# Decode attention with a gated MLP on one core: moving the output selection behind K's second turn, P's copies between the turns, head maxima onto VectorE

## The chip, the cores and the metric

The kernel runs on 1 core of one Trainium2 chip. The metric is device microseconds of a run, as a median of several runs. Besides that time there is one profiled execution of each kernel, whose "span" (first to last instruction) is about 2 us shorter than the run's time.

Engines in the profile: PE is TensorE (matmul), PEld its weight loads, DVE is VectorE, ACT is ScalarE, POOL is GpSimd, SPq is the SyncE queue that issues the loads. QK(g) is the product of the queries with K tile g, PV(g) the product of the softmax's result P with V tile g; PSUM is the memory that the matmuls write (psb in the lines); the kernel uses it in banks. A batch boundary is the step from one batch's last K tile to the next batch's first.

## The reference, cut to what matters

```python
# x: 4 x 1 x 576; 32 query heads, 16 KV heads, head size 128; window of 4096 of 16384 positions
q = layernorm(x) @ wq
k = k_cache[:, :, -4096:, :]; v = v_cache[:, :, -4096:, :]     # each KV head serves two query heads
p = softmax((q @ k.T) * 128 ** -0.5)
h = x + (p @ v) @ wo
gate, up = layernorm(h) @ W_gate, layernorm(h) @ W_up          # 576 x 4608
out = h + (relu(gate) * up) @ W_down
```

All weights and caches are bf16. The window of K and V is 4 batches x 16 heads x 4096 x 128 x 2 bytes x 2, that is 134 MB of the 159.8 MB that the profile counts. Each is used once, so the work is a stream of loads.

## The kernel before: the parts that the change touches

K and V come in 16 tiles each of 4 MiB: tile g has the four KV heads `4*(g%4)` and up of batch `g//4`. They go into four slots, in the order K(g), V(g-4), K(g+1), V(g-3) and so on. So K(g) takes the slot of K(g-2) and its load can be issued only when QK(g-2) has finished; V(g-4) takes the slot of V(g-6) and waits for PV(g-6).

A K tile is turned by VectorE (the kernel's addressing takes a turn as a transposition of blocks of 32x32), in place and in two halves of 128x4096 f32 that take 4.43 us each, before QK can use it:

```python
def turn_k(g, w):                       # w: which half
    ...
    dve(("TRA", g, w), lambda e: e.transpose(out=dst, in_=src), [("L", "K", g)] if w == 0 else [])
def pe_qk(g):   # 32 matmuls; waits for ("TRA", g, 1); of a new batch also for EXP, MAX, EV of the old one
    ...
```

After a batch's fourth QK the softmax follows. The kernel takes the maximum of each row on VectorE and then the maximum over the four rows of a head: with a matmul that lays the 128 maxima in one row, a reduction, a copy, and another matmul that spreads them again:

```python
def head_max(b):
    pe (("MT", b), ... matmul(m_ps[0:1, 0:128], lhsT=stat[:, b, 0:1], rhs=ident_f) ..., [("MAX", b), ...])
    dve(("GM", b), ... tensor_reduce(min) ...);  dve(("GM1", b), ... tensor_copy ...)
    pe (("MB", b), ... matmul(m_ps[:, 0:1], lhsT=gm4[0:1, :], rhs=scl[0:1, 0:1]) ..., [("GM1", b), "c_scl"])
    dve(("NB", b), ... tensor_copy(out=stat[:, b, 1:2], in_=m_ps[:, 0:1]) ..., [("MB", b)])
```

`exps` then computes P, VectorE turns it, `remap` moves it with 16 small matmuls and copies the result to `pT` (four copies on ScalarE, `EV 0`; four on VectorE, `EV 1`). PV(g) multiplies P with a V tile into four PSUM banks; `select_o(g)` picks the wanted entries out of these banks: two products from PSUM (`OSD`), one from SBUF (`OS`), one sum (`OSEL`). PV(g+1) waits for `OSD(g)`, as it writes the same banks. `weights(b)` computes the softmax's divisors once per batch, with two matmuls. The order in which all this is put in the engines' queues is the loop:

```python
def do_v(g):
    pe_pv(g)
    if qd == 0: late.append(lambda: weights(b))
    late.append(lambda: select_o(g))
for g in range(NTILE):
    turn_k(g, 0)
    if g == 4:
        soft(0); remap(0)
    flush()                              # runs what is in late: the selection of V tile g-5
    turn_k(g, 1)
    pe_qk(g)
    if g % 4 == 3 and g > 3: soft(g // 4)
    if g >= 4: do_v(g - 4)
    if g % 4 == 3 and g > 3: remap(g // 4)
for g in range(NTILE - 4, NTILE):
    do_v(g); flush()
```

In the traces below the instructions of an engine start in this order (K7's second turn starts behind the selection at 134.64 us, though its data were there at 122.52), so a place in the order is a possible wait.

## Time and profile before

| | before |
|---|---|
| time, median of 3 runs (range) | 405.31 us (403.62 to 405.83) |
| span of the profiled execution | 403.2 us |
| bytes, mean rate over the span | 159.8 MB, 396 GB/s |
| busy: TensorE, VectorE, ScalarE | 216.4, 228.0, 54.2 us |

No engine is busy for more than 57% of the span. The page's two rows over 40 slices of 10.08 us show what DMA does, first as busy tenths, then as GB/s:

```profile
DMA  9999999999999999769999999399999997999990
GB/s 361 419 416 462 418 419 452 429 419 434 440 423 423 452 421 419 325 260 416 410 427 424 436 423 436 128 419 413 423 423 436 434 429 328 395 417 411 418 403 10
```

The row is near 425 except for the slices 17 and 18 (325 and 260), 26 (128) and 34 (328), counted from 1, and the ends. Cutting the span at these places gives the table of stretches (columns: from and to, length, busy time and number of instructions of each engine, granted TensorE clock with 1.00 as full speed, DMA share, GB/s):

```profile
core 0: us, PE busy (x) PEld busy (x) DVE busy (x) ACT busy (x) POOL busy (x), PEclk, DMA share, GB/s
10.00:168.50 158.50, 69.88 (x476) 11.70 (x236) 106.33 (x69) 25.01 (x35) 7.84 (x13) 0.75 1.00 430
168.50:176.00 7.50, 6.06 (x42) 0.94 (x19) 5.76 (x3) 0.00 (x0) 0.00 (x0) 0.63 0.24 79
176.00:253.50 77.50, 40.16 (x240) 6.01 (x101) 46.48 (x37) 8.49 (x16) 0.00 (x0) 0.77 0.99 424
253.50:262.50 9.00, 6.12 (x43) 0.81 (x19) 7.20 (x3) 0.00 (x0) 0.00 (x0) 0.67 0.27 93
262.50:341.00 78.50, 48.65 (x265) 6.91 (x108) 40.71 (x36) 8.49 (x16) 0.00 (x0) 0.80 0.98 420
341.00:345.20 4.20, 1.99 (x11) 0.78 (x5) 1.96 (x6) 1.16 (x2) 0.00 (x0) 0.94 0.54 164
...
392.80:403.20 10.40, 6.11 (x87) 4.39 (x87) 2.17 (x6) 0.98 (x2) 0.00 (x0) 0.98 0.04 13
```

There are three holes, with 79, 93 and 164 GB/s. The chain that ended last is the list of work, each step released by the one before, that leads to the last instruction. Its first line gives shares by engine, its second by line of the program:

```profile
PE 50%; DVE 36%; DMA 12%; issue 1%; ACT 0%; SPq 0%; DVEq 0%
PE psb L34 29%; DVE sb_arena L442 18%; DMA sb_arena<-in_A_k_cache_dram 12%; PE psb L530 8%; PE psb L466 6%; DVE sb_o_tmp L543 5%; DVE sb_o_sel L547 3%; DVE sb_pp L508 3%; DVE sb_o_tmp L546 2%; DVE sb_stat L471 1%; PE psb L726 1%; PE psb L497 1%; PE psb L646 1%; PE psb L688 1%; PE psb L638 0%
```

DMA has only 12% of this chain; TensorE (PV is at lines 34 and 530, QK at 34 and 466) and VectorE (turn at 442, selection at 543 to 547, P's copies at 508) have 86%. VectorE's timeline around the first batch boundary at which PV runs too, K7 to K8 (called the first from here on; K11 to K12 is the second), shows the chain (columns: start in us, duration, what; in brackets the idle time before it and what ended that):

```profile
122.52 4.45 DVE L442 STREAM_TRANSPOSE sb_arena<-sb_arena 128x4096 f32<-128x4096 f32 x1 [1.91 <-DMA sb_arena<-in_A_k_cache_dram]
131.57 1.38 DVE L543 TENSOR_TENSOR sb_o_tmp<-psb,sb_fm 32x512 f32<-32x512 f32 x2 [4.61 <-PE psb L34]
...
134.64 4.44 DVE L442 STREAM_TRANSPOSE sb_arena<-sb_arena 128x4096 f32<-128x4096 f32 x1
143.03 1.23 DVE L471 TENSOR_REDUCE sb_stat<-psb 128x1 f32<-128x1024 f32 x1 [3.96 <-PE psb L34]
...
155.42 2.73 DVE L508 TENSOR_SCALAR sb_pp<-psb,sb_m 128x512 bf16<-128x512 f32 x4 [7.31 <-PE psb L497]
158.07 4.43 DVE L442 STREAM_TRANSPOSE sb_arena<-sb_arena 128x4096 f32<-128x4096 f32 x1
162.43 1.34 DVE L543 TENSOR_TENSOR sb_o_tmp<-psb,sb_fm 32x512 f32<-32x512 f32 x2
...
165.45 8.76 DVE L442 STREAM_TRANSPOSE sb_arena<-sb_arena 128x4096 f32<-128x4096 f32 x2
```

From 122.52 us: K7's first half is turned as soon as it lands. The selection of V2 waits for PV(2) until 131.57, and only then comes the turn of K7's second half, although K7 had landed twelve us earlier. QK(7) follows and ends at 143.03. P's copies then start at 155.42, after 7.31 us of waiting for the remap, which stands behind PV(3) on TensorE. Only after them come K8's turn, another selection, and the second turn. The line `x2` at 165.45 is K8's second half and K9's first.

The load queue shows the price (columns: start in us, time to issue, what). K10's load waits for QK(8) and leaves at 173.90, 31 us after K9's, and the queue ran dry at about 168.5:

```profile
143.02 0.53 SPq L247 DMA_DIRECT2D sb_arena<-in_A_k_cache_dram  x1
...
173.90 0.53 SPq L247 DMA_DIRECT2D sb_arena<-in_A_k_cache_dram  x1
```

TensorE's timeline at the same place shows the two small matmuls of the head maxima (lines 475 and 482) between QK and PV:

```profile
142.31 0.68 PE L34 MATMUL psb<-sb_arena 128*32 128x512 bf16 x4
144.31 0.38 PE L475 MATMUL psb<-sb_ident_f,sb_stat 128*1 128x128 f32 x2 [1.32 <-DVE sb_stat L471]
145.31 0.38 PE L482 MATMUL psb<-sb_scl,sb_gm 1*128 1x1 f32 x2 [0.62 <-DVE sb_gm L480]
145.62 0.39 PE L530 MATMUL psb<-sb_arena,sb_pp 128*128 128x512 bf16 x1
...
146.71 1.47 PE L34 MATMUL psb<-sb_arena,sb_pp 128*128 128x512 bf16 x3
...
150.98 0.81 PE L34 MATMUL psb<-sb_arena,sb_pp 128*128 128x512 bf16 x3
```

QK ends at 143.0 and PV starts at 145.62, 2.6 us later. Some of PV's matmuls, from 146.7 to 150.1 us, then ran at half the rate: 1.47 us against 0.81 us for three.

From the list of waits (columns: who waited for whom, us in total, times, longest), VectorE waits mostly for TensorE and hardly for loads:

```profile
DVE sb_o_tmp L543 <- PE psb L34: 54.7, 9, 7.0
DVE sb_arena L442 <- DMA sb_arena<-in_A_k_cache_dram: 12.2, 8, 2.4
```

The 72 matmuls of the down projection run without a break at the end, so they waited for computing and not for their weights:

```profile
395.55 4.59 PE L726 MATMUL psb<-sb_arena,sb_pp 128*32 128x288 bf16 x72
```

### The profile page before, as it was taken

Reading aid. Unit: us, or ns where it says so; the run is one execution under the profiler, and the core shown is the slowest. Engines: PE = TensorE matmul, PEld = TensorE weight load, DVE = VectorE, ACT = ScalarE, POOL = GpSimd, SP = SyncE. Lnnn points to the kernel's source line nnn. Section 1 sums busy time; section 2 is a strip of 40 time slices with the busy share of each in tenths; the row PEclk is TensorE's granted clock in tenths of the full one; section 3 lists DMA queues with packets and bytes.
Section 4 is the critical chain, followed back from the end, with each engine's and each line's share of the span. In section 5 each row is a group of like instructions: output and inputs, shape, how many; then the busy total and the mean of one; then the engine's idle time right before and its main releaser. Section 6 shows DMA issues by size and latency. Waiting matters only on the chain.

```text
span 403.2 us, 2703 instructions
## 1 busy us (share of the span) xinstructions
PE 216.4 (54%) x1495; PEld 40.9 (10%) x727; DVE 228.0 (57%) x202; ACT 54.2 (13%) x89; POOL 16.2 (4%) x39
## 2 busy tenths in 40 slices
PE   0403334182829284191927380555473768787676
PEld 0100000010101010010100010010010101100424
DVE  3279978756574735939393629838466322334221
ACT  3290000301010113000001013010101130012110
POOL 8700000000000000000000000000000000000000
PEclk9956886577779779586869596686879698899769
DMA  9999999999999999769999999399999997999990
GB/s 361 419 416 462 418 419 452 429 419 434 440 423 423 452 421 419 325 260 416 410 427 424 436 423 436 128 419 413 423 423 436 434 429 328 395 417 411 418 403 10
DMA packets 6660, 159.76 MB, mean 396 GB/s; under 512 B 748, under 2 KB 888, under 8 KB 1528
## 3 DMA queue, kind: packets, MB, share of 16 engines
q1 hardware_dynamic: 6632, 159.59, 93.0%
q8 instruction: 9, 0.15, 0.1%
q14 instruction: 3, 0.02, 0.0%
q10 hardware_dynamic: 16, 0.01, 0.0%
HBM read 159.58 MB, written 0.00 MB: 396 GB/s over the span
## 4 chain that ended last, share of the span: by engine, by line
PE 50%; DVE 36%; DMA 12%; issue 1%; ACT 0%; SPq 0%; DVEq 0%
PE psb L34 29%; DVE sb_arena L442 18%; DMA sb_arena<-in_A_k_cache_dram 12%; PE psb L530 8%; PE psb L466 6%; DVE sb_o_tmp L543 5%; DVE sb_o_sel L547 3%; DVE sb_pp L508 3%; DVE sb_o_tmp L546 2%; DVE sb_stat L471 1%; PE psb L726 1%; PE psb L497 1%; PE psb L646 1%; PE psb L688 1%; PE psb L638 0%
## 5 line engine op out<-in xcount | busy, mean ns | idle before, releaser
L442 DVE STREAM_TRANSPOSE sb_arena<-sb_arena 128x4096 f32<-128x4096 f32 x32 | 141.0, 4430 | 12.2 <-DMA sb_arena<-in_A_k_cache_dram 12.2
L466 PE MATMUL psb<-sb_arena 128*32 128x512 bf16 x256 | 42.2, 628 | 137.4 <-DVE sb_arena L442 137.4
L34 PE MATMUL psb<-sb_arena,sb_pp 128*128 128x512 bf16 x384 | 108.9, 394 | 0.0
L530 PE MATMUL psb<-sb_arena,sb_pp 128*128 128x512 bf16 x128 | 50.9, 398 | 9.3 <-DVE sb_o_tmp L543 9.3
L543 DVE TENSOR_TENSOR sb_o_tmp<-psb,sb_fm 32x512 f32<-32x512 f32 x32 | 21.7, 678 | 55.0 <-PE psb L34 54.7
L540 ACT COPY sb_o_tmp<-psb 32x512 f32<-32x512 f32 x32 | 18.5, 578 | 204.5 <-PE psb L34 204.2
L34 PE MATMUL psb<-sb_arena 128*32 128x512 bf16 x256 | 44.1, 652 | 0.0
L466 PEld LDWEIGHTS psb<-sb_arena 128*32 128x32 bf16 x256 | 9.7, 120 | 179.6 <-DVE sb_arena L442 150.6
L530 PEld LDWEIGHTS psb<-sb_arena,sb_pp 128*128 128x128 bf16 x128 | 12.9, 101 | 113.6 <-issue 113.6
L508 DVE TENSOR_SCALAR sb_pp<-psb,sb_m 128x512 bf16<-128x512 f32 x16 | 10.9, 744 | 21.5 <-PE psb L497 21.5
L547 DVE TENSOR_REDUCE sb_o_sel<-sb_o_tmp 128x128 f32<-128x512 f32 x16 | 16.3, 1021 | 0.5
L487 ACT ACTIVATE sb_pp<-psb,sb_stat 128x512 bf16<-128x512 f32 x8 | 5.4, 683 | 80.7 <-DVE sb_stat L483 80.7
L556 DVE RECIPROCAL sb_stat<-psb 128x1 f32<-128x1 f32 x4 | 0.7, 168 | 25.9 <-PE psb L554 25.9
L511 ACT ACTIVATE sb_pp<-psb,sb_m 128x512 bf16<-128x512 f32 x16 | 9.7, 688 | 22.7 <-PE psb L497 22.7
L471 DVE TENSOR_REDUCE sb_stat<-psb 128x1 f32<-128x1024 f32 x4 | 4.9, 1225 | 11.9 <-PE psb L34 11.9
L546 DVE TENSOR_TENSOR sb_o_tmp<-sb_o_tmp,sb_fm 64x512 f32<-64x512 f32 x16 | 11.0, 689 | 0.5
L433 ACT COPY sb_arena<-sb_q_keep 32x256 bf16<-32x256 bf16 x8 | 9.7, 1450 | 0.1
L491 DVE STREAM_TRANSPOSE sb_pp<-sb_pp 128x512 bf16<-128x512 bf16 x8 | 5.5, 711 | 3.4 <-ACT sb_pp L487 3.4
L419 DVE CAST sb_pp<-psb 128x512 bf16<-128x512 f32 x1 | 2.4, 2426 | 8.3 <-PE psb L398 8.3
L34 PE MATMUL psb<-sb_arena,sb_hnT 128*32 128x384 bf16 x80 | 6.0, 383 | 0.0
L497 PE MATMUL psb<-sb_pp,sb_to_v 128*32 128x256 bf16 x64 | 4.3, 402 | 2.5 <-DVE sb_pp L491 2.5
L688 PE MATMUL psb<-sb_arena,sb_hnT 128*32 128x384 bf16 x40 | 4.0, 383 | 2.2 <-DVE sb_hnT L669 2.2
(135 smaller groups left out, 95.1 us busy)
## 6 DMA issues: line engine op xcount, KB each, us to landing
sb_arena<-in_A_k_cache_dram SPq DMA_DIRECT2D x16, 4096.0 KB, 17.2
sb_arena<-in_A_v_cache_dram SPq DMA_DIRECT2D x16, 4096.0 KB, 16.8
sb_arena<-in_A_wo_dram SPq DMA_DIRECT2D x1, 4608.0 KB, 13.6
sb_arena<-in_B_W_gate_dram SPq DMA_DIRECT2D x1, 4608.0 KB, 15.9
sb_arena<-in_A_wq_dram SPq DMA_DIRECT2D x1, 4096.0 KB, 12.2
sb_arena<-in_B_W_down_dram SPq DMA_DIRECT2D x3, 1296.0 KB, 19.8
sb_arena<-in_B_W_up_dram SPq DMA_DIRECT2D x1, 3456.0 KB, 16.7
sb_arena<-in_B_W_up_dram SPq DMA_DIRECT2D x1, 1152.0 KB, 19.1
```

The lines of the kernel that those rows point to most:

```text
L34: return e.add_instruction(mybir.InstMatmult(name=e.bass.get_next_instruction_name(), engine=mybir.EngineType.PE, ins=[e.lower_ap(rhs), e. ...
L433: act("QW", lambda e, i=i, q=q: e.copy(out=bass.AP(tensor=arena, offset=32 * i * AW + 2 * i + q, ap=[[AW, 32], [512, 16], [136, 4], [32, 4]]),
L442: dve(("TRA", g, w), lambda e: e.transpose(out=dst, in_=src), [("L", "K", g)] if w == 0 else [])
L466: fn = lambda e, out_=out_, lhsT=lhsT, rhs=rhs, start=start, stop=stop: e.matmul(out_, lhsT=lhsT, rhs=rhs, start=start, stop=stop, skip_gr ...
L471: dve(("MAX", b), lambda e: e.tensor_reduce(out=stat[:, b, 0:1], in_=psb[:, 0:2, :].rearrange("p a b -> p (a b)"), axis=AX.X, op=ALU.max, ...
L508: dve(("EV", b, 1), lambda e, out_=out_, src=src, a=a: e.tensor_scalar(out=out_, in0=src, scalar1=m4[:, a:a + 1], scalar2=None, op0=ALU.mu ...
L511: act(("EV", b, 0), lambda e, out_=out_, src=src, a=a: e.activation(out=out_, in_=src, func=ACT.Copy, scale=m4[:, a:a + 1]), deps + (["c_m ...
L530: fn = lambda e, lhsT=lhsT, rhs=rhs, k=k, j=j: e.matmul(bank[2 + j], lhsT=lhsT, rhs=rhs, start=(k == 0), stop=(k == 7), skip_group_check=True)
L540: act(("OSC", g), lambda e, j=j: e.copy(out=o_tmp[32 * j:32 * j + 32, 0:512], in_=bank[2 + j][32 * j:32 * j + 32, :]), [("PV", g), ("OSEL" ...
L543: dve(("OSD", g), lambda e, j=j: e.tensor_tensor(out=ot(32 * j, 32), in0=bank[2 + j][32 * j:32 * j + 32, :].rearrange("p (t d) -> p t d", ...
L546: dve(("OS", g), lambda e: e.tensor_tensor(out=ot(64, 64), in0=ot(64, 64), in1=fmb(64, 64), op=ALU.mult), [("OSC", g)])
L547: dve(("OSEL", g), lambda e: e.tensor_reduce(out=o_sel[:, qd, b, :], in_=o_tmp[:, 0:512].rearrange("p (t d) -> p d t", d=DH), axis=AX.X, o ...
```

## The change

Its intent is to unchain VectorE from TensorE. The selection goes behind the turn of K's second half, so that QK(g) no longer waits for PV(g-5). P's remap and copies go between the two turns of the next K tile, where a turn fills the wait for the remap. The head maxima are found on VectorE alone by two turns of a 128x32 array. The softmax's divisors take one matmul instead of two. The core of the diff:

```diff
-            pe(("MT", b), lambda e: e.matmul(m_ps[0:1, 0:128], lhsT=stat[:, b, 0:1], rhs=ident_f[:, :], ...
-            ... (GM reduces 1 x 128, GM1 copies 1 x 128)
-            pe(("MB", b), lambda e: e.matmul(m_ps[:, 0:1], lhsT=gm4[0:1, :], rhs=scl[0:1, 0:1], ...
-            dve(("NB", b), lambda e: e.tensor_copy(out=stat[:, b, 1:2], in_=m_ps[:, 0:1]), [("MB", b)])
+            dve(("MT", b), lambda e: e.transpose(out=hy[:, :], in_=hx[:, :]), [("MAX", b)])
+            ... (GM reduces 128 x 32, GM1 copies 128 x 32)
+            dve(("MB", b), lambda e: e.transpose(out=hx[:, :], in_=hy[:, :]), [("GM1", b)])
+            dve(("NB", b), lambda e: e.tensor_scalar(out=stat[:, b, 1:2], in0=hx[:, 0:1], scalar1=SCALE, ...
 ...
-            pe(("LS", b), lambda e: e.matmul(m_ps[:, 0:1], lhsT=sameh..., rhs=stat[:, b, 13:14], ...
-            dve(("RL", b), lambda e: e.reciprocal(out=stat[:, b, 14:15], in_=m_ps[:, 0:1]), [("LS", b)])
-            dve(("FQ", b), lambda e: e.tensor_scalar(out=fq, in0=qm, scalar1=stat[:, b, 14:15], ...
+            dve(("FQ", b), lambda e: e.tensor_scalar(out=fq, in0=qm, scalar1=stat[:, b, 13:14], ...
             pe(("F4M", b), ... the mask toq now also sums over the four rows of a head ...
-            dve(("F4", b), lambda e: e.tensor_copy(out=f4[:, :], in_=m_ps[:, 0:4]), [("F4M", b)])
+            dve(("F4", b), lambda e: e.reciprocal(out=f4[:, :], in_=m_ps[:, 0:4]), [("F4M", b)])
 ...
             turn_k(g, 0)
             if g == 4:
                 soft(0)
-                remap(0)
+            if g and g % 4 == 0:
+                remap(g // 4 - 1)
+            turn_k(g, 1)
             flush()
-            turn_k(g, 1)
             pe_qk(g)
             if g % 4 == 3 and g > 3:
                 soft(g // 4)
             if g >= 4:
                 do_v(g - 4)
-            if g % 4 == 3 and g > 3:
-                remap(g // 4)
+        remap(B - 1)
+        flush()
```

Left out: the masks that are no longer needed (`ident_f`, `sameh`, `scl`), the new buffers, and twelve more mask operations on GpSimd at the start.

More of the change, by code (lines that the diff above doesn't have):

```diff
@@ L153, in bass_sequential_preLN__sliding_block_cached__glu_gated_reglu__decode_kernel @@
         ident_b = sb("ident_b", [128, 128], BF16)
-        ident_f = sb("ident_f", [128, 128], FP32)
         ones_d = sb("ones_d", [128, 128], FP32)
@@ L167, in bass_sequential_preLN__sliding_block_cached__glu_gated_reglu__decode_kernel @@
         e8 = sb("e8", [128, 8], FP32)
-        sameh = sb("sameh", [128, 16, 4, 2], FP32)
         toq = sb("toq", [128, 16, 4, 2], FP32)
@@ L183, in bass_sequential_preLN__sliding_block_cached__glu_gated_reglu__decode_kernel @@
         stat = sb("stat", [128, B, 16], FP32)
-        gmh = sb("gmh", [1, 32], FP32)
-        gm4 = sb("gm4", [1, 128], FP32)
-        scl = sb("scl", [1, 1], FP32)
+        hx = sb("hx", [128, 32], FP32)
+        hy = sb("hy", [128, 32], FP32)
+        gmh = sb("gmh", [128, 8], FP32)
         fq = sb("fq", [128, 4], FP32)
@@ L303, in bass_sequential_preLN__sliding_block_cached__glu_gated_reglu__decode_kernel @@
         pool("c_qW", lambda e: e.memset(arena[:, 0:QWW].bitcast(FP32), 0.0))
-        pool("c_idf0", lambda e: e.memset(ident_f[:, :], 0.0))
-        pool("c_idf", lambda e: e.affine_select(out=ident_f[:, :], in_=ident_f[:, :], pattern=[[-1, 128]],
-                                                compare_op=ALU.not_equal, fill=1.0, base=0, channel_multiplier=1), ["c_idf0"])
-        pool("c_scl", lambda e: e.memset(scl[:, :], SCALE))
+        pool("c_hx", lambda e: e.memset(hx[:, :], 0.0))
         pool("c_onesd", lambda e: e.memset(ones_d[:, :], 1.0 / D))
@@ L330, in bass_sequential_preLN__sliding_block_cached__glu_gated_reglu__decode_kernel @@
         pool("c_selc0", lambda e: e.memset(selc[:, :, :, :], 0.0))
-        pool("c_same0", lambda e: e.memset(sameh[:, :, :, :], 0.0))
-        for j in range(4):
-            pool(f"c_same{j + 1}", lambda e, j=j: e.affine_select(out=sameh[:, :, :, :], in_=sameh[:, :, :, :],
-                                                                pattern=[[-8, 16], [0, 4], [-1, 2]], compare_op=ALU.not_equal,
-                                                                fill=1.0, base=-2 * j, channel_multiplier=1), [f"c_same{j}"])
         pool("c_toq0", lambda e: e.memset(toq[:, :, :, :], 0.0))
-        for q in range(4):
+        for q in range(16):
             pool(f"c_toq{q + 1}", lambda e, q=q: e.affine_select(out=toq[:, :, :, :], in_=toq[:, :, :, :],
                                                                pattern=[[0, 16], [-32, 4], [-1, 2]], compare_op=ALU.not_equal,
-                                                               fill=1.0, base=-8 * q, channel_multiplier=1), [f"c_toq{q}"])
+                                                               fill=1.0, base=-2 * q, channel_multiplier=1), [f"c_toq{q}"])
         pool("c_xs0", lambda e: e.memset(xsel[:, :], 0.0))
@@ L470, in row_max @@
         def row_max(b):
-            dve(("MAX", b), lambda e: e.tensor_reduce(out=stat[:, b, 0:1], in_=psb[:, 0:2, :].rearrange("p a b -> p (a b)"),
-                                                      axis=AX.X, op=ALU.max, negate=True), [("QK", 4 * b + 3)])
+            dve(("MAX", b), lambda e: e.tensor_reduce(out=hx[:, 0:1], in_=psb[:, 0:2, :].rearrange("p a b -> p (a b)"),
+                                                      axis=AX.X, op=ALU.max, negate=True), [("QK", 4 * b + 3), "c_hx", ("NB", b - 1) if b else None])
@@ L474, in head_max @@
         def head_max(b):
-            pe(("MT", b), lambda e: e.matmul(m_ps[0:1, 0:128], lhsT=stat[:, b, 0:1], rhs=ident_f[:, :], start=True, stop=True),
-               [("MAX", b), ("F4", b - 1) if b else "QT", "qkeep0", "qkeep1", "c_idf"])
-            dve(("GM", b), lambda e: e.tensor_reduce(out=gmh[:, :].rearrange("p (u q) -> p u q", q=2),
-                                                     in_=m_ps[0:1, 0:128].rearrange("p (u i q) -> p u q i", i=4, q=2),
+            dve(("MT", b), lambda e: e.transpose(out=hy[:, :], in_=hx[:, :]), [("MAX", b)])
@@ L479, in head_max @@
+            dve(("GM", b), lambda e: e.tensor_reduce(out=gmh[:, :].rearrange("p (d q) -> p d q", q=2),
+                                                     in_=hy[:, :].rearrange("p (d i q) -> p d q i", i=4, q=2),
                                                      axis=AX.X, op=ALU.min), [("MT", b)])
-            dve(("GM1", b), lambda e: e.tensor_copy(out=gm4[:, :].rearrange("p (u i q) -> p u i q", i=4, q=2),
-                                                    in_=bass.AP(tensor=gmh, offset=0, ap=[[32, 1], [2, 16], [0, 4], [1, 2]])), [("GM", b)])
@@ L482, in head_max @@
-            pe(("MB", b), lambda e: e.matmul(m_ps[:, 0:1], lhsT=gm4[0:1, :], rhs=scl[0:1, 0:1], start=True, stop=True), [("GM1", b), "c_scl"])
-            dve(("NB", b), lambda e: e.tensor_copy(out=stat[:, b, 1:2], in_=m_ps[:, 0:1]), [("MB", b)])
+            dve(("GM1", b), lambda e: e.tensor_copy(out=hy[:, :].rearrange("p (d i q) -> p d i q", i=4, q=2),
+                                                    in_=bass.AP(tensor=gmh, offset=0, ap=[[8, 128], [2, 4], [0, 4], [1, 2]])), [("GM", b)])
@@ L485, in exps @@
+            dve(("MB", b), lambda e: e.transpose(out=hx[:, :], in_=hy[:, :]), [("GM1", b)])
+            dve(("NB", b), lambda e: e.tensor_scalar(out=stat[:, b, 1:2], in0=hx[:, 0:1], scalar1=SCALE, scalar2=None, op0=ALU.mult),
+                [("MB", b)])
         def exps(b):
@@ L553, in weights @@
                 [("EXP", b, 0), ("EXP", b, 1)])
-            pe(("LS", b), lambda e: e.matmul(m_ps[:, 0:1], lhsT=sameh[:, :, :, :].rearrange("p u i q -> p (u i q)"), rhs=stat[:, b, 13:14],
-                                             start=True, stop=True), [("WL", b), ("NB", b), "c_same4"])
-            dve(("RL", b), lambda e: e.reciprocal(out=stat[:, b, 14:15], in_=m_ps[:, 0:1]), [("LS", b)])
-            dve(("FQ", b), lambda e: e.tensor_scalar(out=fq[:, :], in0=qm[:, :], scalar1=stat[:, b, 14:15], scalar2=None,
-                                                     op0=ALU.mult), [("RL", b), "c_qm"])
+            dve(("FQ", b), lambda e: e.tensor_scalar(out=fq[:, :], in0=qm[:, :], scalar1=stat[:, b, 13:14], scalar2=None,
+                                                     op0=ALU.mult), [("WL", b), "c_qm"])
             pe(("F4M", b), lambda e: e.matmul(m_ps[:, 0:4], lhsT=toq[:, :, :, :].rearrange("p j t h -> p (j t h)"), rhs=fq[:, :],
-                                              start=True, stop=True), [("FQ", b), "c_toq4"])
-            dve(("F4", b), lambda e: e.tensor_copy(out=f4[:, :], in_=m_ps[:, 0:4]), [("F4M", b)])
+                                              start=True, stop=True), [("FQ", b), "c_toq16", "QT", "qkeep0", "qkeep1"])
+            dve(("F4", b), lambda e: e.reciprocal(out=f4[:, :], in_=m_ps[:, 0:4]), [("F4M", b)])
             dve(("FM", b), lambda e: e.tensor_tensor(
```

## The prediction

> **What bounds the kernel now.** The page: span 403.2 us, 159.8 MB, 396 GB/s on average. The table of stretches shows DMA at 420 to 431 GB/s except in three holes: 168.5 to 176 us (79 GB/s), 253.5 to 262.5 (93), 341 to 345.2 (164). Against 425 GB/s they lose about 6, 7 and 2.6 us, 15.7 together. Ahead of the first hole each K tile's first turn waits for its load every 19.43 us; two 4 MiB loads in that time are 432 GB/s[...]. So DMA is the limit, except where buffers come free too late.
>
> Why they do: the chain of waits repeats, per K tile, end of PV(g-5), selection on VectorE (3.1 us), turn of K's second half (4.4), QK on TensorE (4.2), PV(g-4) (6.9). That ring is 18.6 us, hardly under 19.4, so QK ends about 20.6 us after its K tile lands and lateness is not made up. At a batch boundary QK, maxima, two tiny matmuls, PV, P's remap, P's copies, turn, selection, turn follow one another: QK(7) ends at 143.0, QK(8) at 174, and the load that needs QK(8)'s buffer is issued at 173.9, after the queue ran dry.
>
> **What the change does.**
> 1. Selection after the second half's turn: QK(g) no longer waits for PV(g-5); the selection runs beside QK. The ring breaks; per tile VectorE has 12 us, TensorE 11, DMA 19.4. QK should end about 13 us after K lands (8.8 + 4.2), 7 earlier. This is the main part.
> 2. P's copies (2.7 us) go after the next K tile's first turn. Today VectorE stands 7.3 and 5.7 us before them, behind PV and the remap; a 4.4 us turn fills that. I expect QK(8) some 16 us after K8's landing; the slots forgive about 29 (three loads) less the 13 us of other work.
> 3. Head maxima on VectorE: two 32x32 turns and three small operations, estimated at 0.2 us each, replace 1.7 us with two trips to TensorE; PV no longer queues behind them. About 1 us a batch, invisible once DMA is the limit.[...]
> 4. Weights: one matmul and a reciprocal's wait go; twelve more mask operations on POOL are off the path.
>
> **The sum.** All three holes close: 15.7 us. The tail changes owner: today compute ends late (DMA data end at 393, the down projection runs 395.6 to 400.2). With DMA the limit, output projection and gate/up should be about 10 us ahead of the last weights, so the end is last landing plus about 4 us (last down matmuls, eviction, 2.6 us store), saving 4 to 5 more. Span about 382; measured time is 2 us more. **384 us, 8 in 10 between 380 and 390.** Faster by over 2%: 0.95; within 2%: 0.04; slower: 0.01.
>
> **Signs.** DMA at 420 GB/s or more in every slice but first and last; the chain's largest share on DMA, not PE and VectorE; turns waiting for K loads; QK right after the turn; the last down matmuls waiting for the last weight load.
>
> **What would make it wrong.** A hole at the batch boundary remains because the remap still queues behind PV (then 388 to 394); denser TensorE work lowers the granted clock (0.79 now) and lengthens PV; loads slow beside the turns; the tail stays bound by compute.

15.7 us of holes and 4 to 5 of tail, taken from the span of 403.2 us, give 382.5 to 383.5, put as "about 382", and 2 us more give the 384 us. That DMA is the limit rests on the 432 GB/s and the turns' waits for their loads. The 0.2 us for each operation of the maxima are the author's estimate; in the trace of before, three small operations of the maxima on VectorE (lines 477, 480 and 483) took 0.28, 0.21 and 0.16 us, and no turn of 128x32 had been timed. The 2.6 us of the store are there too, from its issue at 400.62 us to the end of the span.

## The result, and the profile after

| | before | after |
|---|---|---|
| time, median (range) | 404.47 us (403.36 to 405.83, 4 runs) | 380.13 us (379.85 to 381.31, 4 runs) |
| ratio | 1 | 0.9402 (95% interval 0.9362 to 0.9442) |
| span | 403.2 us | 378.4 us |
| mean rate over the span | 396 GB/s | 422 GB/s |
| busy: TensorE, VectorE | 216.4, 228.0 us | 213.3, 230.6 us |
| mean granted TensorE clock | 0.788 | 0.815 |

A ratio here is the mean time of one kernel's runs over that of the other's in the same rounds, so it is not quite the ratio of the medians.

The engines do nearly the same work as before, in 24.8 us less. The two DMA rows, now with slices of 9.46 us:

```profile
DMA  8999999999999999999999999999999999999994
GB/s 333 443 441 429 414 433 440 443 426 416 435 434 443 423 421 436 436 440 419 423 436 436 436 423 429 435 436 433 423 429 438 429 436 423 441 421 422 416 426 190
```

The holes are gone; only the first and the last slice are thin. In the table of stretches, 360 us without a break run at 430 GB/s:

```profile
10.00:370.00 360.00, 210.05 (x1425) 36.33 (x657) 226.83 (x190) 50.52 (x83) 13.49 (x20) 0.81 1.00 430
370.00:378.40 8.40, 2.82 (x40) 1.58 (x36) 0.45 (x1) 0.39 (x1) 0.00 (x0) 1.00 0.41 164
```

The chain that ended last has changed its owner. DMA had 12% of it and now has 61%:

```profile
DMA 61%; PE 19%; DVE 15%; issue 4%; SPq 1%
```

VectorE's timeline at the same batch boundary:

```profile
122.50 8.77 DVE L431 STREAM_TRANSPOSE sb_arena<-sb_arena 128x4096 f32<-128x4096 f32 x2 [7.37 <-DMA sb_arena<-in_A_k_cache_dram]
131.31 1.38 DVE L532 TENSOR_TENSOR sb_o_tmp<-psb,sb_fm 32x512 f32<-32x512 f32 x2
...
135.21 1.22 DVE L460 TENSOR_REDUCE sb_hx<-psb 128x1 f32<-128x1024 f32 x1 [0.61 <-PE psb L34]
136.46 0.21 DVE L464 STREAM_TRANSPOSE sb_hy<-sb_hx 128x32 f32<-128x32 f32 x1
...
141.99 4.46 DVE L431 STREAM_TRANSPOSE sb_arena<-sb_arena 128x4096 f32<-128x4096 f32 x1 [2.22 <-DMA sb_arena<-in_A_k_cache_dram]
146.37 2.69 DVE L497 TENSOR_SCALAR sb_pp<-psb,sb_m 128x512 bf16<-128x512 f32 x4
148.96 4.44 DVE L431 STREAM_TRANSPOSE sb_arena<-sb_arena 128x4096 f32<-128x4096 f32 x1
```

K7 lands at 122.50 as before, but both its halves are turned at once (8.77 us) and the selection comes afterwards. QK(7) ends at 135.2 and not at 143.0. The head maxima are a handful of operations of about 0.2 us. K8 lands at 141.99, and now VectorE waits for it (2.22 us here, 0.9 to 7.4 us before the tiles from K4 on). P's copies follow the first turn at 146.37 without waiting. The queue answers:

```profile
135.20 0.53 SPq L245 DMA_DIRECT2D sb_arena<-in_A_k_cache_dram  x1
...
157.35 0.54 SPq L245 DMA_DIRECT2D sb_arena<-in_A_k_cache_dram  x1
```

QK(8) has ended at 157.35 and K10's load leaves then, eleven us before the moment at which the queue ran dry in the kernel before. In the list of waits the same lines as before have changed places:

```profile
DVE sb_arena L431 <- DMA sb_arena<-in_A_k_cache_dram: 63.8, 16, 7.4
DVE sb_o_tmp L532 <- PE psb L34: 18.1, 3, 7.2
```

And the last matmuls wait for the last weights, in two steps of 18 matmuls:

```profile
366.92 3.26 PE L713 MATMUL psb<-sb_arena,sb_pp 128*32 128x288 bf16 x36
372.00 1.28 PE L713 MATMUL psb<-sb_arena,sb_pp 128*32 128x288 bf16 x18 [1.82 <-DMA sb_arena<-in_B_W_down_dram]
374.06 1.36 PE L713 MATMUL psb<-sb_arena,sb_pp 128*32 128x288 bf16 x18 [0.77 <-DMA sb_arena<-in_B_W_down_dram]
```

### The profile page after: what moved, and what is told of

The parts are those of the page before. It is cut to its first block, busy times and chain, and to the rows that moved or that the text cites. A ratio compares the mean times of both kernels' runs of the same rounds, so it can differ in the third digit from the quotient of the medians.

```text
span 378.4 us, 2668 instructions
## 1 busy us (share of the span) xinstructions
PE 213.3 (56%) x1471; PEld 38.3 (10%) x703; DVE 230.6 (61%) x206; ACT 54.2 (14%) x89; POOL 21.9 (6%) x44
## 4 chain that ended last, share of the span: by engine, by line
DMA 61%; PE 19%; DVE 15%; issue 4%; SPq 1%
DMA sb_arena<-in_A_k_cache_dram 52%; DVE sb_arena L431 13%; PE psb L34 11%; DMA sb_arena<-in_B_W_down_dram 9%; PE psb L455 4%; PE psb L519 3%; DVE sb_o_tmp L532 1%; DVE sb_pp L497 1%; PE psb L545 0%; PE psb L713 0%; SPq L245 0%; PE psb L486 0%; SPq L287 0%; DVE sb_fq L543 0%; DVE sb_out_sb L716 0%
## 5 line engine op out<-in xcount | busy, mean ns | idle before, releaser
L431 DVE STREAM_TRANSPOSE sb_arena<-sb_arena 128x4096 f32<-128x4096 f32 x32 | 140.7, 4429 | 63.8 <-DMA sb_arena<-in_A_k_cache_dram 63.8
L34 PE MATMUL psb<-sb_arena,sb_pp 128*128 128x512 bf16 x384 | 106.6, 387 | 0.0
L455 PE MATMUL psb<-sb_arena 128*32 128x512 bf16 x256 | 44.3, 639 | 107.3 <-DVE sb_arena L431 107.3
L519 PE MATMUL psb<-sb_arena,sb_pp 128*128 128x512 bf16 x128 | 50.2, 392 | 9.3 <-DVE sb_o_tmp L532 9.3
L34 PE MATMUL psb<-sb_arena 128*32 128x512 bf16 x256 | 45.1, 643 | 0.0
L519 PEld LDWEIGHTS psb<-sb_arena,sb_pp 128*128 128x128 bf16 x128 | 12.7, 99 | 115.0 <-issue 115.0
L536 DVE TENSOR_REDUCE sb_o_sel<-sb_o_tmp 128x128 f32<-128x512 f32 x16 | 17.7, 1104 | 0.5
L329 POOL TENSOR_SCALAR_AFFINE_SELECT sb_toq<-sb_toq 128x128 f32<-128x128 f32 x16 | 12.6, 788 | 2.3
L500 ACT ACTIVATE sb_pp<-psb,sb_m 128x512 bf16<-128x512 f32 x16 | 9.8, 697 | 12.7 <-PE psb L486 12.7
L545 PE MATMUL psb<-sb_fq,sb_toq 128*128 128x4 f32 x8 | 1.8, 301 | 12.2 <-DVE sb_fq L543 12.2
L713 PE MATMUL psb<-sb_arena,sb_pp 128*32 128x288 bf16 x72 | 5.9, 319 | 2.6 <-DMA sb_arena<-in_B_W_down_dram 2.6
L684 DVE TENSOR_TENSOR sb_pp<-psb,sb_pp 128x384 bf16<-128x384 f32 x3 | 1.5, 551 | 8.4 <-PE psb L675 8.4
```

What stands on the lines that cost most here:

```text
L34: return e.add_instruction(mybir.InstMatmult(name=e.bass.get_next_instruction_name(), engine=mybir.EngineType.PE, ins=[e.lower_ap(rhs), e. ...
L329: pool(f"c_toq{q + 1}", lambda e, q=q: e.affine_select(out=toq[:, :, :, :], in_=toq[:, :, :, :], pattern=[[0, 16], [-32, 4], [-1, 2]], com ...
L455: fn = lambda e, out_=out_, lhsT=lhsT, rhs=rhs, start=start, stop=stop: e.matmul(out_, lhsT=lhsT, rhs=rhs, start=start, stop=stop, skip_gr ...
L500: act(("EV", b, 0), lambda e, out_=out_, src=src, a=a: e.activation(out=out_, in_=src, func=ACT.Copy, scale=m4[:, a:a + 1]), deps + (["c_m ...
L519: fn = lambda e, lhsT=lhsT, rhs=rhs, k=k, j=j: e.matmul(bank[2 + j], lhsT=lhsT, rhs=rhs, start=(k == 0), stop=(k == 7), skip_group_check=True)
L536: dve(("OSEL", g), lambda e: e.tensor_reduce(out=o_sel[:, qd, b, :], in_=o_tmp[:, 0:512].rearrange("p (t d) -> p d t", d=DH), axis=AX.X, o ...
```

## The experiments

Theory A says that in the kernel before, the ring of selection, second turn, QK and PV kept QK late, and that breaking it leaves DMA as the only limit. Rival B says that only batch boundaries mattered, above all the place of P's copies. Rival C says that the head maxima's trips through TensorE did it. The record marks all of these kernels as correct, even the one that is wrong (experiment 7), so this mark says little about errors in attention. The times of the kernel before in the same rounds are given with each. The changed kernel was timed in other rounds (before: 404.47 us there, 403.11 to 403.54 here), so differences of about 1 us from its 380.13 us say nothing.

### 1. The selection's place alone (sel_only)

```diff
             if g == 4:
                 soft(0)
                 remap(0)
-            flush()
             turn_k(g, 1)
+            flush()
```

> The kernel before, with nothing changed but the place of the selection (after the turn of the second half of K). Theory A (the ring of selection, turn, QK and PV kept QK late; breaking it gives back all the slack): QK of the first K tile of a batch still ends about 22 us after that tile lands, under the 25 to 27 us that the slots forgive, so no hole in DMA and 380 to 382 us, 98% or more of the gain. Rival B (holes are made at batch boundaries, by P's copies standing behind PV; the selection's place only shifts work): the holes stay, two of them above 3 us, and the time is 393 to 400 us. Rival C (trips of the head maxima through TensorE): about the time before, 400 to 404.

Measured: 380.59 us (before 403.34), ratio 0.9448 (0.9418 to 0.9479). This one moved line gives 22.8 us, and no hole is left:

```profile
GB/s 333 443 433 429 414 440 443 433 422 422 438 437 429 426 422 441 440 426 426 426 439 433 429 426 433 435 429 436 422 436 433 428 436 422 443 421 417 422 425 190
```

The first QK of the new batch ends at 161.46, about 19.4 us after its K tile landed (if that came one period of 19.43 us after K7's 122.61), although P's copies still stand 5.65 us waiting behind PV, and the small matmuls are still there. Rivals B and C fall as explanations of the whole: with the ring broken, what they name costs nothing that the times can tell. The gain isn't the steady ring alone: K10's load leaves 12.4 us earlier than in the trace of before (161.46 against 173.90), of which 7.6 us were there when QK(7) ended (135.38 against 143.02). The other 4.8 us come at the boundary, where 3.1 us of selection no longer stand between K8's two turns, and where the wait before P's copies is 1.7 us shorter (5.65 against 7.31) because PV(3) did not run at half rate in this trace: the V load that waits for PV(3) leaves 9.71 us after QK(7)'s end (135.38 to 145.09), against 11.39 us in the trace of before (143.02 to 154.41).

### 2. The place of P's copies alone (copies_only)

```diff
             if g == 4:
                 soft(0)
-                remap(0)
+            if g and g % 4 == 0:
+                remap(g // 4 - 1)
             flush()
             turn_k(g, 1)
 ...
-            if g % 4 == 3 and g > 3:
-                remap(g // 4)
+        remap(B - 1)
```

> The kernel before, with nothing changed but the place of P's remap and copies (between the two turns of the next K tile); the selection stays before the second turn. Theory A: the ring of 18.6 us stays, so lateness is hardly made up; each boundary costs 4.4 us less (a turn fills the wait). First hole 0 to 2 us, second about 5: 394 to 399 us. Rival B: all holes go, 380 to 383 us. Rival C: 400 to 404.

Measured: 393.15 us (before 403.34), ratio 0.9756. That is 10.2 us, a little more than expected. Holes remain in slices 18, 20 and 26:

```profile
GB/s 332 442 432 436 447 425 429 429 429 431 430 425 429 429 429 431 432 382 429 362 426 431 429 429 432 283 436 409 415 429 422 431 432 402 407 426 417 408 419 43
```

VectorE's timeline at the second boundary shows the mechanism as predicted: the turn stands before the copies and the wait is down to 1.32 us.

```profile
231.36 4.40 DVE L442 STREAM_TRANSPOSE sb_arena<-sb_arena 128x4096 f32<-128x4096 f32 x1
237.08 2.73 DVE L508 TENSOR_SCALAR sb_pp<-psb,sb_m 128x512 bf16<-128x512 f32 x4 [1.32 <-PE psb L497]
```

The time from the end of a batch's last QK to the end of the next batch's first one, read from the two K loads that they release, is 251.21 - 226.35 = 24.9 us at this boundary, against 260.34 - 231.11 = 29.2 us in the kernel before. That is 4.4 us, the length of the turn. At the first boundary the same reading gives 168.81 - 143.98 = 24.8 us against 173.90 - 143.02 = 30.9, 6.0 us less: there PV(3)'s stretch at half rate in the trace of before adds 1.7 us. The two make 10.4 us, near the 10.2 measured.

### 3. Head maxima and weights alone (small_only)

The kernel before's loop, with the changed `head_max`, `weights` and masks.

> The kernel before, with nothing changed but head maxima on VectorE and the shorter weights. Theory A: PV starts about 2.7 us earlier after QK at each of three boundaries, and as these stand in the chain of a hole each hole gets shorter by about that: 395 to 399 us; DMA still has holes. Rival B: nothing, 403 to 405. Rival C: most of the gain, 380 to 388.

Measured: 391.53 us (before 403.34), ratio 0.9705, so 11.8 us: more than theory A expected, and far from nothing. The holes are smaller, not gone:

```profile
GB/s 326 437 444 433 432 430 433 433 440 433 426 430 430 430 428 427 430 396 430 427 434 425 433 430 433 217 433 427 437 430 430 422 430 440 412 420 418 419 387 5
```

### 4. The selection put back (sel_back)

The changed kernel with `flush()` before `turn_k(g, 1)` again.

> The changed kernel, with the selection put back before the turn of the second half (so P's copies and the small parts without the selection's move). Theory A: ring of 18.6 us stays; per boundary only 4.4 + 2.7 us less than before: first boundary at the edge of what the slots forgive, second a hole of 1 to 3 us, 383 to 389 us. Rival B: 380 to 381, no loss. If the parts simply added up, the loss would be what the selection alone gains.

Measured: 383.01 us (before 403.34), ratio 0.951. This is 20.3 us, nearly the sum of experiments 2 and 3 (10.2 + 11.8 = 22.0). The hole of 1 to 3 us that theory A expected isn't visible in the loads (first line; the second is the chain that ended last):

```profile
GB/s 330 440 440 436 434 419 426 426 440 440 434 430 419 429 426 438 440 436 433 419 430 424 440 436 433 431 422 429 429 440 436 431 433 421 437 426 426 410 420 54
PE 46%; DVE 38%; DMA 13%; issue 1%; ACT 1%; SPq 0%; DVEq 0%
```

But the chain that ended last is still TensorE 46% and VectorE 38%, with DMA at 13%: this kernel still ends on the chain of the two engines, which is just little slower than the loads. So the parts overlap. The selection alone gives 22.8 us, everything else without it 20.3 us, and together they give 24.3 us in their own rounds, because the loads allow no more (430 GB/s over 360 us in the changed kernel).

### 5. The two small parts, one at a time (max_only, weights_only)

The prediction said that head maxima give "about 1 us a batch". Experiment 3 said otherwise, so each part was tried alone on the kernel before.

> The kernel before with head maxima on VectorE alone (weights as before). The prediction said about 1 us a batch; the two small parts together gave 11.8 us. Reading of the traces: the matmul and the broadcast of the maxima hold PV back 2.7 us behind QK at three batch boundaries, and the first batch's QK comes 0.9 us earlier, so 3 times 2.7 plus 0.9 is 9.0 us less than the kernel before, about 394.3 us. If the prediction's 1 us a batch were right: 399 to 400 us.

Measured: 395.18 us (before 403.54), ratio 0.9797 (0.977 to 0.9825), 8.4 us less; the interval includes 2%, so whether it is over 2% stays open.

> The kernel before with the shorter weights alone (head maxima as before). Reading of the traces: the first K tile after a batch's first PV comes 0.7 to 1.0 us earlier in four batches (a matmul, its reciprocal and one product leave the wait between PV and the selection), so 3 to 4 us less than before, 399.5 to 400.5 us. If the parts are not additive, or the gain sits in the maxima alone: 402.5 to 404 us.

Measured: 399.59 us (before 403.54), ratio 0.9886 (0.9834 to 0.9939), 4.0 us less; one of its four runs, at 395.96 us, lies apart from the others, and without it the median is 3.4 us less. That is a gain clear of the noise, but within 2%. The sum of 12.4 us agrees with the 11.8 us of experiment 3. By the traces, the larger share is that PV no longer starts 2.6 us after QK (in the trace of after, which has the same head maxima, PV's first matmul starts at 135.09 us, before the load that waits for QK(7) leaves at 135.20): three boundaries make 7.8 us. This share wasn't tested apart.

### 6. More work for VectorE (extra4, extra9)

```diff
-            dve(("TRA", g, w), lambda e: e.transpose(out=dst, in_=src), ...)
+            dve(("TRA" if w == 0 or g < 4 else "TRB", g, w), lambda e: e.transpose(out=dst, in_=src), ...)
+            if w == 1 and g >= 4:
+                part_ = k[:, 0:2048]                        # extra9: 0:4096
+                dve(("TRC", g), lambda e: e.transpose(out=part_, in_=part_), [("TRB", g, 1)])
+                dve(("TRA", g, 1), lambda e: e.transpose(out=part_, in_=part_), [("TRC", g)])
```

The two added turns undo one another, so the result stays right. A form of these two kernels, without the waits between the turns, had a race.

> The changed kernel, with two more turns of half a half-tile (in place, they undo one another) for each K tile from the fifth on: VectorE gets about 4.4 us more per tile, 53 us in all, in the stretch where QK waits. If DMA alone is the limit there (theory A): per tile VectorE has 16.4 of 19.4 us, QK ends 17.6 us after K's landing, no hole: 380 to 382 us. If VectorE or the chain through QK still sets the pace: tens of us more, up to 430.

Measured: 382.33 us (before 403.11), ratio 0.9471. VectorE is busy for 285.4 us instead of 230.6, and the time is only 2.2 us over the changed kernel's. This is 0.3 us above the expected range, and the slices show where it is lost, in the tenth and eleventh:

```profile
GB/s 331 440 438 437 430 415 430 437 434 382 394 430 440 440 440 432 427 409 437 440 440 436 430 423 416 440 439 437 437 423 420 426 440 437 430 433 416 414 427 143
```

Against 430 GB/s these lose 1.1 and 0.8 us. K6's load, which waits for QK(4), left late here:

```profile
90.19 0.54 SPq L245 DMA_DIRECT2D sb_arena<-in_A_k_cache_dram  x1
```

In the changed kernel it left at 85.14. So the very first batch boundary, where softmax, copies and both turns of K4 follow one another, had less than 5 us of room; I had looked at the later ones only. At these no hole of this size appears; the lowest slice there has 409 GB/s.

> The changed kernel, with two more turns of a whole half-tile for each K tile from the fifth on: about 8.8 us more per tile, 20.8 of 19.4 us. Now VectorE is over DMA's time: 12 tiles of 20.8 plus three batch boundaries of about 5 us are 265 us against 233 us of loads, of which about 14 us are forgiven by the slots: 393 to 402 us, with holes in DMA again. This shows where the room ends.

Measured: 423.73 us (before 403.11), ratio 1.0518: slower than the kernel before, and 22 us above my range.

VectorE is over the loads' time per tile, as meant, and has 67% of the chain that ended last. The estimate failed in two terms. The work took longer: from K4's landing (64.25) to the end of QK(15) (about 341) it is 277 us and not 265. And nothing of "14 us are forgiven" was seen. The last K load leaves at 298.65, 46 us later than in the changed kernel (252.62), and the end comes 45.4 us later. From this load to the end it takes 125.2 us here, 125.8 us in the changed kernel and 123.0 us in the kernel before. What follows the last K tile is a chain of computing nearly as long as the loads that remain, so lateness at the last K tile is passed on to the end and not forgiven.

### 7. Less work for TensorE (light_pv)

```diff
-            for k in range(8):
+            for k in (0, 7):
```

The result is wrong. The check doesn't see three quarters of PV missing.

> The changed kernel with a quarter of PV's matmuls (wrong result on purpose): TensorE has about 80 us less. Theory A (DMA alone is the limit): 378.5 to 380.5 us, no faster than 1.5 us below the changed kernel. If TensorE or its granted clock still held something back: 5 us or more below.

Measured: 380.54 us (before 403.11), ratio 0.9438 (0.9414 to 0.9462). TensorE's busy time falls from 213.3 to 135.5 us and the time doesn't move. PV now waits for its V tiles (the columns of a group: line, engine, operation, shape and count; busy us, mean ns; idle us before it and what ended it):

```profile
L519 PE MATMUL psb<-sb_arena,sb_pp 128*128 128x512 bf16 x25 | 11.4, 455 | 16.1 <-DMA sb_arena<-in_A_v_cache_dram 16.1
```

With experiment 6 this brackets the limit: 78 us less on TensorE gives nothing, and 55 us more on VectorE costs 2.2 us. The mean granted clock was 0.682, lower than the changed kernel's 0.815, although TensorE had less to do.

### 8. A finer tail (fine_tail)

```diff
-for r0, r1 in ((0, 9),) if j < 3 else ((0, 6), (6, 8), (8, 9)):
+for r0, r1 in ((0, 9),) if j < 2 else ((0, 5), (5, 9)) if j == 2 else ((0, 3), (3, 6), (6, 8), (8, 9)):
 ... (the matmuls' waits are placed to match)
```

> The changed kernel with the last two of four down-projection loads cut finer (0 to 5, 5 to 9; 0 to 3, 3 to 6, 6 to 8, 8 to 9), so that fewer of the last matmuls wait for the last load. In the trace of after the last 18 matmuls (1.36 us) all start at 374.06 us, on the landing of the 864 KB piece. Expected 0.3 to 1.0 us less than the changed kernel, 379.1 to 379.8 us; [...]no difference, or 0.5 us more by more issues.

Measured: 380.09 us (before 403.11), ratio 0.9427 (0.9404 to 0.945). The last group of matmuls is only six, but it starts at 374.50 instead of 374.06 us, as the last landing itself decides (the group waits 0.19 us for its load). The last matmul ends 0.3 us earlier in the trace (375.14 against 375.42), but no gain can be told from the changed kernel's 380.13 us, so the expected 0.3 to 1.0 us is neither shown nor excluded at its lower end. The times fit the other outcome, no difference. Its 0.5 us is about the time of one issue, 0.53 to 0.54 us for a K load in the traces. No version that beats the changed kernel was found: 360 us of its 378.4 run at 430 GB/s.

## Why the prediction was right or wrong

The time, 380.13 us, lies in the predicted range of 380 to 390 but at its very edge, 3.9 us below the predicted 384. The changed kernel's four runs go from 379.85 to 381.31 us, so that the median fell inside the range by 0.13 us is luck. The direction and the mechanism were right, several sizes were not.

- **What bounds the kernel.** Right. The trace of after has 430 GB/s over 360 us, with VectorE busy for 226.8 us of them. Experiments 6 and 7 show that neither VectorE nor TensorE bounds the changed kernel while it streams. Of the signs, one failed narrowly: four inner slices have less than 420 GB/s (414 to 419). The others came as predicted.
- **Step 1, the ring and its breaking.** Right, and shown by experiment 1. "QK should end about 13 us after K lands": it was 12.7 us (122.50 to 135.2), before 20.5. "This is the main part": alone it gives 22.8 us, partly because it shortens the boundaries too (experiment 1). What the prediction left out is that the other parts would give nearly as much without it (20.3 us).
- **Step 2, P's copies.** Right in size: 4.4 us were saved at the second boundary in experiment 2, and QK(8) came 15.4 us after K8's landing, predicted 16. But in the changed kernel this part isn't needed: experiment 1 reaches the same time without it.
- **Step 3, head maxima, "about 1 us a batch".** Mis-sized. I counted the shorter path of the maxima and named, but didn't price, that PV no longer queues behind them. PV started 2.6 us earlier at each of three boundaries, and the part alone is worth 8.4 us. "Invisible once DMA is the limit" was right. The 32x32 blocks are how the kernel is written; no run tries another size. In the trace of after a turn of 128x32 f32 took 213 ns, one of 128x512 bf16 712 ns and one of 128x4096 f32 4429 ns; between the two f32 sizes this is 1.04 ns per column, and the bf16 turn lies on the same line.
- **Step 4, weights.** Its size wasn't given; alone it is worth 4.0 us.
- **The sum.** The terms were 15.7 us of holes and 4 to 5 us of tail. The tail was right: at the mean rates of the last stretches, data of about 0.3 us were left in the last 10.4 us before, and 3.2 us in the last 8.4 us after, so 10.1 us without data became 5.2, 4.9 us less. The down projection now waits for its weights, and gate/up ended at 363.4 us, 10.7 us before the last group of matmuls could start on its weights, as predicted. The term that failed is the price of the lost time. I valued holes against 425 GB/s, the mean of the good stretches. Two of these were themselves thinned by late loads (424 and 420 GB/s; the first 24 us after the first hole have 411, the last 13.5 before the second 437), where the undisturbed rate is 430. At 430, the holes are 15.8 us and these two stretches 2.9 us more. With the tail this makes 23.6 us of the 24.8 us between the two spans; 1.2 us are not assigned.
- **"Denser TensorE work lowers the granted clock."** This fear, a guess that no trace had shown, did not come true. The profiled executions have 0.788 before and 0.815 after. Over all runs it is 0.783 to 0.812 before and 0.797 to 0.830 after, so there is no sign of a fall, and the rise isn't clear of the spread. With a third of TensorE's work taken away it was lower, 0.682 to 0.707. What sets the clock, the runs don't show. In the trace of before, three of PV's matmuls took 1.47 us shortly after the pause for the head maxima, and three others took 0.81 us four us later. The same 2.6 us between QK and PV, with two small matmuls in them, came before half the rate at the first and third batch boundaries (granted clock 0.50 from 146.7 to 150.1 us and from 320.8 to 324.2) and not at the second (1.00 from 235.3 to 238.7), so the pause alone does not explain it.

## What to carry to other kernels

When the chain that ended last goes to and fro between two engines and the loads have only 12% of it, time taken out of that chain can count nearly in full, even from operations of 0.2 us (here 8.4 us where 9.0 were read from the trace), until the loads become the limit; then the parts of a change stop adding up, and each has to be tried alone to know what it is worth. Look for the one wait that closes the ring: here it was the order of two instructions on VectorE, and moving one line gave nearly everything. Price lost load time at the rate of an undisturbed stretch, not at the mean of all that look good (here 430 against 425 GB/s).
